# A chunked linear recurrence with an MLP mixer behind it: the recurrence rewritten for quarter tiles of TensorE

## The chip, the cores and the metric

One core of one Trainium2 chip. The time is what the device takes for one execution, in microseconds (us), the lower the better. Engines are named as in the profile: PE is TensorE (PEld its weight load), DVE is VectorE, ACT is ScalarE, POOL is GpSimd, SP is SyncE, which issues most transfers.

## The reference

For each of 4 batches and 8 heads a 40x40 state runs over 768 tokens. The outputs of the heads, side by side, are the input of an MLP mixer.

```python
B, H, S, D = r.shape                      # 4, 8, 768, 40
for t in range(S):
    y[:, :, t] = np.einsum('bhd,bhde->bhe', rt, state)
    Sa = np.einsum('bhde,bhe->bhd', state, at)
    state_decay = state * wt[:, :, None, :] - np.einsum('bhd,bhe->bhde', Sa, bt)
    state = state_decay + np.einsum('bhd,bhe->bhde', vt, kt)

x = y as (B, S, H * D)                    # 320 columns
h = np.maximum(x.transpose(0, 2, 1) @ w_tok1, 0.0) @ w_tok2
u = x + h.transpose(0, 2, 1)
out = u + np.maximum(u @ w_ch1, 0.0) @ w_ch2
```

All inputs and the output are fp32.

## The kernel before

Time is cut into 48 chunks of 64 tokens (g, 12 per batch), heads into four pairs (p). Within a chunk the recurrence is done with matrices. With decays folded into r, a, k and b by cumulated products, the chunk needs the 64x64 lower triangles of A·K and A·B, the inverse T of one plus the second, and from these the outputs and the state that the next chunk starts from. The work is written as generator tasks:

- **t_pre(q)**, once per pair of chunks: cumulated products of w (scans, L443 and L540), multiplied into a (tile AB) and into k and b (tile KBp) by DVE, POOL or ACT (`either`, L370); the correction P of the output; the decay of a whole chunk, PC.
- **t_a(g)**: px (L648) = the products of AB with KBp for two heads at once, a 128x128 matrix whose diagonal 64x64 blocks matter; pa (L614), a transposed by a selection matrix; pk (L270), k and b transposed, evicted into KT and stored to DRAM, from where t_load reads it back as KB. From px come the masked triangle in AT (mask `low`, DVE, L658), and for the inverse the blocks Dg (ACT, L674) and N (L666).
- **t_solve**: inverts the 32x32 diagonal blocks of eight chunks at a time (six sets) on DVE, into TBt and TBn. In the first two sets (`pem=2`) it inverts 16x16 blocks and **merge** (L864, 48 small matmuls a chunk) completes them on PE.
- **t_b(g)**: two products with 32x32 tiles (pe L912, pt L940) complete the 64x64 inverse in TBD, with copies L904 to L906 and L946; ph (L956) multiplies AT by it: HU, evicted by ACT at L961.
- **t_chain(0), t_chain(1)**: the recurrence itself, in two groups of four heads. pq (L1014) goes into a PSUM bank, ACT copies it to G (L1021); four matmuls of HU with G follow, one head after another in one column half (pr, L1027) up to chunk 15, two heads side by side in both halves (pr2, L1033) from chunk 16 on. ACT takes W2s from that (L1070 to L1075), DVE the masked RM (L1043, L1059, L1060, L1065). pS (L1088 and L1089, from chunk 12 on L1097 and L1099 in both halves) gives the new state, DVE multiplies it by PC into the next G (L1107 to L1110), pU (L270) transposes it, ACT copies it to VSs (L1126).
- **t_y**, every second chunk: the outputs of two chunks, L1153 (KB, RM) and L1155 (VSs, RBs), in one PSUM bank yb; DVE multiplies by P (L1185).
- **t_mlp**, once per batch behind its last chunk's output: 1152 records of L1533 and 864 of L1422 in the page are most of it. **t_piece** converts its weights in the first third.

All matmuls of the recurrence are fp32. One fp32 matmul leaves two records in the trace, each with its own weight load. A matmul on fewer rows or columns than 128 uses a tile of the array. What the profile writes as 104\*64 is a matmul with 104 rows, 64 columns.

The order of each engine is static. A planner (class Planner) runs the tasks before the program is built, with a cost for every instruction and a rank (the chunk number less an offset from table K); each engine takes the ready instruction of lowest rank. PSUM banks are rings: three of kind w (evicted by preparation), two of kind c (chain), two of kind m (MLP), one of kind y. On PE the planner inserts filler matmuls (L357, to yb) where too few columns have streamed. All engines thus run a fixed list, and an instruction that waits holds up what is behind it on its engine.

```python
def rank_a(g): ...        # rank of t_a
yield g - K["chain"]      # t_chain, rank of chunk g
yield rank - K["mrg"]     # merge
```

## Time and profile before

| | |
|---|---|
| runs | 937.53, 944.76 and 950.08 us, median 944.76 |
| span of the profiled execution | 933.5 us |
| PE busy | 868.9 us, 93% |
| PEld busy | 807.2 us, 86% |
| DVE busy | 645.8 us, 69% |
| ACT busy | 471.5 us, 51% |
| POOL busy | 256.3 us, 27% |

The time of a run holds some 11 us that lie around the span. Busy time is the union of an engine's instructions; PE's overlap, so their durations do not add up, and what a group costs is read from the start of one group to the start of the next. The granted clock (PEclk) is the share of full speed that PE's clock was allowed.

The program's parts follow each other roughly like this: up to about 100 us the first set is solved; to about 300 us batch 0's recurrence runs beside preparation and weight conversion; then the MLP of one batch runs beside the recurrence of the next; the last product of an output with P starts at 842.8 us, and what follows is the last batch's channel mixing.

### The profile page before, as it was taken

What the parts mean: (1) busy time and instruction counts of PE and PEld (TensorE: products, weight loads), DVE (VectorE), ACT (ScalarE), POOL (GpSimd) and SP (SyncE); (2) the same over time, 40 slices, a digit from 0 to 9 for tenths busy, and PEclk for the clock granted to TensorE, in tenths of its full rate; (3) what the DMA queues carried; (4) which work ended last, traced back from release to release, by engine and by line L of the source; (5) the groups of instructions that cost most, each with busy time, mean ns of one, the idle gap of its engine ahead of it and who ended that gap; (6) DMA issues with size and microseconds to landing.
All of it is one profiled execution on the core that took longest, in us unless ns stands there. A gap on an engine that the chain in (4) does not pass through costs nothing.

```text
span 933.5 us, 28874 instructions
## 1 busy us (share of the span) xinstructions
PE 868.9 (93%) x11662; PEld 807.2 (86%) x11662; DVE 645.8 (69%) x1504; ACT 471.5 (51%) x1501; POOL 256.3 (27%) x335
## 2 busy tenths in 40 slices
PE   4887799998998899999999999999999999998997
PEld 4877697887987888999899888989999999998997
DVE  5789667885888896799836988667975534444443
ACT  2554575655778346546735654554446344433221
POOL 7344533453565312134411121101211111100000
PEclk9788688977999899999859999999999999999999
DMA  5653456547758845454666743644256344335432
GB/s 129 160 163 124 137 166 177 148 120 205 205 178 241 240 128 153 128 131 112 176 179 201 195 138 95 189 106 130 82 172 196 122 117 136 85 101 166 167 99 84
DMA packets 134100, 139.59 MB, mean 150 GB/s; under 512 B 84360, under 2 KB 116872, under 8 KB 130888
## 3 DMA queue, kind: packets, MB, share of 16 engines
q1 hardware_dynamic: 127624, 90.47, 35.3%
q0 software_dynamic: 6336, 47.19, 15.8%
q8 instruction: 95, 1.56, 0.7%
q14 instruction: 45, 0.37, 0.1%
HBM read 111.08 MB, written 26.54 MB: 147 GB/s over the span
## 4 chain that ended last, share of the span: by engine, by line
PE 67%; DMA 11%; DVE 8%; issue 6%; POOL 3%; ACT 3%; SPq 1%; POOLq 0%; DVEq 0%; ACTq 0%
PE m L1422 15%; PE m L1533 13%; DMA w<-in_wT_dram 5%; PE px L648 4%; PE ph L956 4%; PE pq L1014 4%; PE pa L614 4%; PE pq L1033 3%; PE yb L1153 2%; PE yb L1155 2%; PE pt L940 2%; PE pk L270 2%; PE pq L1027 2%; PE pe L912 2%; PE pm L864 2%
## 5 line engine op out<-in xcount | busy, mean ns | idle before, releaser
L1533 PE MATMUL m<-ut,wg_c 128*128 128x256 f32 x1152 | 176.9, 295 | 0.4 <-DVE hd L1545 0.2
L1533 PEld LDWEIGHTS m<-ut,wg_c 128*128 128x128 f32 x1152 | 151.6, 193 | 4.7 <-DVE x L1573 0.4
L1422 PE MATMUL m<-wg_c,hd 128*128 128x320 f32 x864 | 152.3, 317 | 2.7 <-DVE hd L1545 2.3
L1422 PEld LDWEIGHTS m<-wg_c,hd 128*128 128x128 f32 x864 | 128.0, 188 | 6.1 <-DVE hd L1545 3.5
L1543 ACT ACTIVATE hd<-m 128x256 fp32r<-128x256 f32 x144 | 55.3, 384 | 123.8 <-PE m L1533 122.8
L1545 DVE SCALAR_TENSOR_TENSOR hd<-m,hd 128x256 fp32r<-128x256 f32 x144 | 60.6, 421 | 62.1 <-ACT hd L1543 61.8
L906 POOL COPY TBD<-TBt 32x128 f32<-32x128 f32 x86 | 43.9, 510 | 165.7 <-PE ph L956 118.6
L1573 DVE TENSOR_TENSOR x<-m,x 128x320 f32<-128x320 f32 x96 | 46.8, 487 | 53.0 <-PE m L1422 52.5
L370 POOL TENSOR_TENSOR cv_c<-cv_c 128x320 f32<-128x320 f32 (+3 forms) x63 | 61.9, 997 | 69.9 <-ACT cv_c L1257 51.6
L674 ACT ACTIVATE Dg<-px 128x128 f32<-128x128 f32 x144 | 56.1, 390 | 21.0 <-PE px L648 19.2
L1014 PE MATMUL pq<-RBs,VSs 104*104 104x128 f32 x384 | 65.6, 301 | 0.8 <-POOL VSs L1000 0.7
L1043 POOL TENSOR_TENSOR RM<-G,upp 64x128 f32<-64x128 f32 x43 | 22.8, 534 | 143.5 <-ACT G L1021 113.0
L956 PE MATMUL ph<-TBD,AT 128*104 128x128 f32 x384 | 59.2, 299 | 0.9 <-ACT TBD L946 0.6
L648 PE MATMUL px<-KBp,AB 104*128 104x128 f32 x384 | 58.3, 301 | 1.8 <-DVE AT L607 1.6
L1014 PEld LDWEIGHTS pq<-RBs,VSs 104*104 104x104 f32 x384 | 53.6, 188 | 2.5 <-POOL VSs L1000 0.9
L648 PEld LDWEIGHTS px<-KBp,AB 104*128 104x128 f32 x384 | 52.7, 212 | 2.8 <-DVE AT L607 1.8
L1356 POOL DMA_DIRECT2D wg_c<-sG x32 | 18.0, 564 | 131.3 <-PE m L1533 58.4
L956 PEld LDWEIGHTS ph<-TBD,AT 128*104 128x104 f32 x384 | 50.4, 186 | 3.6 <-ACT TBD L946 1.0
L443 DVE TENSOR_TENSOR_SCAN w<-w,D 104x512 f32<-104x512 f32 x24 | 35.1, 1461 | 25.9 <-DMA w<-in_wT_dram 25.9
L614 PE MATMUL pa<-sel,AB 104*128 104x40 f32 x384 | 52.0, 288 | 0.0
L614 PEld LDWEIGHTS pa<-sel,AB 104*128 104x128 f32 x384 | 51.4, 208 | 0.2
L1153 PE MATMUL yb<-KB,RM 128*64 128x40 f32 x768 | 51.3, 235 | 0.0
(179 smaller groups left out, 1980.2 us busy)
## 6 DMA issues: line engine op xcount, KB each, us to landing
wg_c<-sG POOLq DMA_DIRECT2D x16, 1152.0 KB, 6.1
wg_c<-sG POOLq DMA_DIRECT2D x16, 960.0 KB, 5.3
KBp<-in_kbT_dram SPq DMA_DIRECT2D x24, 416.0 KB
wg_t<-sT POOLq DMA_DIRECT2D x8, 1152.0 KB, 6.1
sKB<-KT SPq DMA_DIRECT2D x48, 160.0 KB
KB<-sKB SPq DMA_DIRECT2D x48, 160.0 KB
wr<-in_wT_dram SPq DMA_DIRECT2D x24, 208.0 KB
w<-in_wT_dram SPq DMA_DIRECT2D x24, 208.0 KB
```

The lines of the kernel that those rows point to most:

```text
L370: return [(e, Port(60 + f * n / 0.96 if e == "DVE" else 140 + 2.24 * n), lambda e=e: engines[e].tensor_tensor(out=out_(), in0=a_(), in1=b_ ...
L614: return ("PE", (109, 208, "A"), lambda: nc.tensor.matmul(d["pa"][:, p, :], lhsT=ab[:, p, :], rhs=sel, start=True, stop=True))
L648: nc.tensor.matmul(d["px"][:, p, :], lhsT=ab[:, p, :], rhs=KBp[q][:, p, z, :], start=True, stop=True)
L674: return ("ACT", 190 if sl.start == 0 else 392, lambda: nc.scalar.activation(out=Dg[sl, :, ci * NP:(ci + 1) * NP].rearrange("p s n -> p n s"),
L956: nc.tensor.matmul(d["ph"][0:DP, p, :], lhsT=at[:, p, :], rhs=d["tbd"][:, p, :], start=True, stop=True)
L1014: nc.tensor.matmul(d["pq"][0:DP, 2 * p:2 * p + 2, D:DP], lhsT=vs[:, gi * 2 + p, :], rhs=rb[:, gi * 2 + p, :].rearrange("p (h t) -> p h t", ...
L1153: nc.tensor.matmul(dst, lhsT=rms[g - 1 + z][:, h, :], rhs=o["kb"][:, h, :], start=True, stop=False)
L1422: nc.tensor.matmul(d[key], lhsT=lhs(i, a_), rhs=rhs(i, b_), start=i == 0 and j == 0, stop=i == n - 1 and j == 2)
L1533: nc.tensor.matmul(pt, lhsT=mm_[q][0], rhs=mm_[q][1], start=q == 0, stop=q == len(mm_) - 1)
L1543: nc.scalar.activation(out=hid[key][:, 0], in_=pt, func=AF.Relu)
L1545: now = yield [("DVE", dve(256), lambda: nc.vector.scalar_tensor_tensor(out=hid[key][:, 1], in0=pt, scalar=0.0, in1=hid[key][:, 0].bitcast ...
L1573: now = yield [("DVE", dve(320), lambda: tt(out=x()[:, i], in0=d[("c2", g, i)], in1=x()[:, i], op=ALU.add))]
```

## The change

The recurrence is written in another form, for all eight heads at once. For a chunk with the state S:

- Z = X·V (xv, L991 of the new kernel) + A·S (as_, L1000), both into one bank of kind c, with X the masked triangle. Its negative ZS is evicted by ACT (L1016) or DVE (L1018).
- U = T·Z (L1030) and its transpose (L1033), in two banks of kind c. U goes into the tile W beside V (L1042 on ACT, L1043 on DVE), its transpose to UT (L1106).
- S update (sm, L1057) from KB and W; DVE adds the old state (L1072) and multiplies by PC (L1076; at a batch's first chunk one multiplication, L1070). pu (L1085) transposes the state, evicted into SS (L1092).
- RM (rr, L1122): products of V and U transposed with r, in two banks of kind w, masked by DVE (L1133), two instructions of 128x256 a chunk.
- y (L1168 and L1171) on four column tiles of 32; the first chunk of a batch has no state term.

So pa, ph and HU, pq and G, W2s, RBs, VSs and the matrices idS, low, uppn and PC2 are gone. px (L658) works once per pair of chunks on tiles of 64 rows and 32 columns, eight matmuls per chunk and head pair, into two banks; the mask is applied to the product (XT, L670, one DVE instruction of 128x512). pe and pt run once per pair of chunks, pe (L928) writing its result twice, pt (L943) with a copy by the identity (L946); TBD is evicted in one instruction (L951 or L952) with a masked copy of TBt by POOL or ACT (L909 to L912). Odd heads lie in the other half of the partitions, so the host lays out a, r, v and k, b padded, and a, r and v come in one transfer each. The merge remains for the first set only (pem=1). PSUM banks are allocated once and cleared at the start (L339), and `banks` takes two of a ring at once. Table K of the planner has new numbers throughout. The MLP's code is unchanged.

Matmuls of the recurrence, records halved: px 1536 (192 before), pe 768, pt 768, xv 384, as_ 352, U and its transpose 384 each, sm 352, pu 352, rr 768, y 1472, merge 384 (768 before).

```diff
         def px(z, p):
             def f():
-                nc.tensor.matmul(d["px"][:, p, :], lhsT=ab[:, p, :], rhs=KBp[q][:, p, z, :], start=True, stop=True)
-            return ("PE", (218, 512, "A"), f)
+                ab = AB[q]
+                for i in range(2):
+                    for hf in range(2):
+                        for r in range(2):
+                            rs = rows(r)
+                            rhs = ab[rs, p, z]
...
+                            o0 = i * 64 + hf * 32
+                            nc.tensor.matmul(d["px"][0 if i == r else 1][0][o0:o0 + 32, z, p, :],
+                                             lhsT=KBp[q][rs, p, z, i, hf * 32:hf * 32 + 32], rhs=rhs, start=True, stop=True)
...
+        def pe(n):
             def f():
-                q0, q1 = h * 64, h * 64 + 32
-                nc.tensor.matmul(d["pe"][q0:q0 + L, p, :], lhsT=n21[q1:q1 + L, p, :],
-                                 rhs=TBt[q1:q1 + L, :, ci * NP + p], start=True, stop=True)
+                for dup in range(2):
+                    for b in range(2):
+                        s0, o0 = slice(b * 64, b * 64 + L), b * 64 + (1 - dup) * L
+                        nc.tensor.matmul(d["pe"][o0:o0 + L, n, :], lhsT=o["n21"][s0, n, :], rhs=TBn[s0, n0 + n, :], start=True, stop=True)
...
-    def t_chain(gi):
+    def t_chain():
+        for g in range(NG):
...
+            def xv(p):
+                def f():
+                    for r in range(2):
+                        b = 1 - r
+                        nc.tensor.matmul(d["z"][b * 64:b * 64 + 64, p, :], lhsT=oq["xt"][r * 64:r * 64 + 64, z, p, :],
+                                         rhs=o["w2"][r * 64:r * 64 + 64, 2 * p + r, :], start=p == 0, stop=c == 0 and p == NP - 1,
+                                         skip_group_check=True)
+                return f
+
+            def as_(p):
+                def f():
+                    for r in range(2):
+                        b = 1 - r
+                        nc.tensor.matmul(d["z"][b * 64:b * 64 + 64, p, :], lhsT=AB[q][rows(r), p, z, :],
+                                         rhs=ST[g][rows(r), p, :], start=False, stop=p == NP - 1, skip_group_check=True)
+                return f
...
+            def uu(p):
+                def f():
+                    for r in range(2):
+                        bs = slice((1 - r) * 64, (1 - r) * 64 + 64)
+                        nc.tensor.matmul(u_[bs, p, 0:D], lhsT=oq["tbd"][bs, z, p, :], rhs=d["zs"][bs, p, :], start=True, stop=True)
+                    for r in range(2):
+                        bs = slice((1 - r) * 64, (1 - r) * 64 + 64)
+                        nc.tensor.matmul(t_[rows(r), p, :], lhsT=d["zs"][bs, p, :], rhs=oq["tbd"][bs, z, p, :], start=True, stop=True)
+                return f
...
+            def sm(p):
+                def f():
+                    for r in range(2):
+                        nc.tensor.matmul(d["s"][rows(r), p, :], lhsT=o["kb"][:, 2 * p + r, :], rhs=o["w2"][:, 2 * p + r, :], start=True, stop=True)
+                return f
...
+        def rr(p):
+            def f():
+                for src, hf in (("vt", 0), ("ut", 1)):
+                    for r in range(2):
+                        o0 = 64 * (r ^ hf)
+                        lhs = o["vt"] if hf == 0 else d["ut"]
+                        nc.tensor.matmul(bk[r][0][o0:o0 + 64, p, :], lhsT=lhs[rows(r), p, :],
+                                         rhs=o["rb"][rows(r), p, r * 64:r * 64 + 64], start=True, stop=True)
+            return f
...
+                            if part == 0:
+                                nc.tensor.matmul(dst, lhsT=RMs[gz][:, h, hf * 32:hf * 32 + 32], rhs=o["kb"][:, h, :], start=True, stop=zero)
+                            else:
+                                t1 = r * 64 + hf * 32
+                                nc.tensor.matmul(dst, lhsT=o["rb"][:, p, t1:t1 + 32], rhs=SS[gz][:, p, :], start=False, stop=True)
```

How the new order looks on PE. A piece of the list before, in batch 0's recurrence: the preparation of one chunk (pk, px, pa) and the chain's pq and pr.

```order
L270 MATMUL pk_2853<-ident,KBp_2566 128x104 x4
L648 MATMUL px_2854<-KBp_2566,AB_113 128x128 x4
L614 MATMUL pa_2788<-sel,AB_113 128x40 x4
L1014 MATMUL pq_1_2780<-RBs_131,VSs_137 104x2x64
L1027 MATMUL pq_0_2775<-G_2590,HU_2547 64x104 x4
```

And of the new list, PE through one chunk of the chain; bkc and bkw are banks of the kinds c and w. Ahead of the piece stands rr.

```order
L1122 MATMUL bkw_118<-RB_6963,UT_7291 64x64
L991 MATMUL bkc_122<-W_6841,XT_4211 64x40 x8
L1000 MATMUL bkc_122<-ST_7385,AB_3725 64x40 x8
L1030 MATMUL bkc_121<-ZS_7447,TBD_6778 64x40 x2
L1033 MATMUL bkc_122<-TBD_6778,ZS_7447 40x64 x2
```

The pair of L1030 and L1033 stands there four times, and then:

```order
L1085 MATMUL bkw_120<-sel,ST_7088 40x40 x8
L1085 MATMUL bkw_119<-sel,ST_7385 40x40 x8
L276 MATMUL bkw_118<-ident,KBp_6648 128x104 x4
L1057 MATMUL bkc_121<-W_6841,KB_6981 40x40 x8
L1168 MATMUL yb<-KB_6496,RM_7327 32x40
```

Four 128x128 matmuls became eight small ones each, and the chain's matmuls stand directly behind each other with the evictions of ZS and W between them, which run on other engines.

On DVE, in the same part of the program, before: RM and the state products of the two groups stand between conversions of the MLP's weights (cv_c).

```order
L1065 TENSOR_TENSOR RM_3140<-pq_0_3101,upp 128x256
L1252 TENSOR_SCALAR cv_c_1_1_3137<-cv_c_1_1_3137 128x320
L1065 TENSOR_TENSOR RM_3140<-pq_1_3142,upp 128x256
L370 TENSOR_TENSOR cv_c_1_0_3075<-cv_c_1_0_3075 128x320
L1110 TENSOR_TENSOR G_3146<-pS_0_3186,PC_130 40x4x40
L1110 TENSOR_TENSOR G_3146<-pS_1_3210,PC_130 40x4x40
```

In the new list DVE masks RM from its two banks, with a decay product of KBp between, and makes the state in two steps (L1072, L1076), with conversions between those too.

```order
L1133 TENSOR_TENSOR RM_3718<-bkw_120,upp 128x4x64
L391 TENSOR_TENSOR KBp_3333<-KBp_3333,wr_3304 104x1024
L1133 TENSOR_TENSOR RM_3718<-bkw_118,upp 128x4x64
L1072 TENSOR_TENSOR ST_3748<-bkc_122,ST_3466 104x160
L1265 TENSOR_SCALAR cv_c_1_1_2989<-cv_c_1_1_2989 128x384
L1076 TENSOR_TENSOR ST_3748<-ST_3748,PC 104x160
L391 TENSOR_TENSOR cv_c_1_1_2989<-cv_c_1_1_2989 128x384
L670 TENSOR_TENSOR XT_3839<-bkw_120,upp 128x512
```

The state now passes DVE twice and may stand behind a conversion in between.

## Rows read from the trace of the kernel before

**Rows 1.** The page, part 1: busy time, share of the span, instructions.
```profile
PE 868.9 (93%) x11662; PEld 807.2 (86%) x11662; DVE 645.8 (69%) x1504; ACT 471.5 (51%) x1501; POOL 256.3 (27%) x335
```

**Rows 2.** Two stretches: length, busy PE, PEld, DVE, ACT, POOL; clock, DMA share, GB/s.
```profile
0.00:300.00 300.00, 259.50 (x4369) 237.09 (x4369) 229.07 (x489) 176.56 (x532) 140.87 (x152) 0.86 0.59 164
300.00:842.00 542.00, 527.39 (x6668) 489.34 (x6669) 379.49 (x929) 273.54 (x907) 110.65 (x175) 0.96 0.50 145
```

**Rows 3.** The second stretch: busy PE and PEld of L648, then of L1033 alone.
```profile
300.00:842.00 542.00, 25.63 (x176) 23.33 (x176) 0.96 0.50 145
...
300.00:842.00 542.00, 32.41 (x512) 24.70 (x512) 0.96 0.50 145
```

**Rows 4.** Short stretches, columns as in rows 2: the clock stands third from the end.
```profile
98.00:99.20 1.20, 1.14 (x65) 1.07 (x66) 1.20 (x5) 0.69 (x2) 0.00 (x0) 0.50 0.61 178
178.00:184.50 6.50, 6.50 (x115) 5.95 (x113) 5.76 (x10) 5.47 (x18) 0.00 (x0) 1.00 0.82 228
186.00:200.00 14.00, 11.26 (x298) 10.38 (x297) 12.33 (x22) 6.44 (x19) 6.66 (x8) 0.63 0.37 104
406.00:411.00 5.00, 5.00 (x133) 4.63 (x132) 4.61 (x13) 1.76 (x7) 2.33 (x1) 1.00 0.01 4
420.00:422.00 2.00, 2.00 (x37) 1.65 (x36) 1.77 (x6) 1.41 (x6) 0.00 (x0) 1.00 0.81 170
```

**Rows 5.** PE's timeline near 180 us: start, duration, line, tile and records.
```profile
179.34 1.16 PE L648 MATMUL px<-KBp,AB 104*128 104x128 f32 x8
180.33 0.98 PE L614 MATMUL pa<-sel,AB 104*128 104x40 f32 x8
181.14 1.10 PE L1014 MATMUL pq<-RBs,VSs 104*104 104x128 f32 x8
182.17 0.62 PE L912 MATMUL pe<-TBt,N 32*32 32x32 f32 x16
182.73 0.93 PE L1027 MATMUL pq<-G,HU 104*64 104x104 f32 x8
183.58 0.22 PE L864 MATMUL pm<-TBt,N 32*32 32x32 f32 x1
...
183.97 0.23 PE L864 MATMUL pm<-TBt,N 32*32 32x32 f32 x1
```

**Rows 6.** PE's timeline near 408 us.
```profile
406.30 0.64 PE L940 MATMUL pt<-ET,TBn 32*32 32x32 f32 x16
406.88 0.28 PE L1097 MATMUL pS<-W2s,KB 128*40 128x40 f32 x4
...
407.52 0.29 PE L1153 MATMUL yb<-KB,RM 128*64 128x40 f32 x4
...
409.49 0.60 PE L270 MATMUL pU<-sel,G 40*40 40x40 f32 x8
410.01 1.12 PE L956 MATMUL ph<-TBD,AT 128*104 128x128 f32 x8
410.89 1.20 PE L1533 MATMUL m<-ut,wg_c 128*128 128x256 f32 x8
```

**Rows 7.** PE's timeline near 420 us.
```profile
420.25 0.93 PE L1033 MATMUL pq<-G,HU 104*64 104x104 f32 x16
421.11 0.62 PE L912 MATMUL pe<-TBt,N 32*32 32x32 f32 x16
```

**Rows 8.** PE's timeline near 98 us.
```profile
98.06 0.68 PE L864 MATMUL pm<-ET,TBn 32*32 32x32 f32 x32 [1.42 <-DVE ET L871]
98.54 0.64 PE L864 MATMUL pm<-TBn,ET 32*32 32x32 f32 x32
99.11 1.14 PE L357 MATMUL yb<-ident 128*128 128x192 bf16 x6
```

**Rows 9.** DVE by line and shape: count, busy us, mean ns, idle time before.
```profile
L658 DVE TENSOR_TENSOR AT<-px,low 128x256 f32<-128x256 f32 x48 | 19.9, 417 | 9.1 <-ACT Dg L674 4.5 <-PE pU L270 2.2 <-ACT noff L666 1.7
L1110 DVE TENSOR_TENSOR G<-pS,PC 40x160 f32<-40x160 f32 x22 | 7.0, 327 | 6.0 <-PE pS L1089 5.6
```

## Prediction before the run

> **What bounds the kernel now.** I read the page's busy shares first. TensorE is busy 93% of the span, VectorE 69%, ScalarE 51%, GpSimd 27% [rows 1]. A share of 93% can still hide stretches with other limits, so the second view is a table of two, cut where the work changes: up to 300 us the recurrence of batch 0 runs beside preparation and weight conversion, up to 842 us recurrence and MLP share the engines; behind that only the MLP of batch 3 is left, 92 us in which nothing of the change runs. From 300 to 842 us TensorE is busy 527 of 542 us at a mean granted clock of 0.96 [rows 2]: there a microsecond of TensorE is a microsecond of the span. Before, it is busy 259.5 of 300 us and VectorE 229, so there VectorE is close behind.
>
> The third view says which chunks fall where: of the px matmuls 176 of 384 records lie behind 300 us, so 22 chunks of 48 are prepared there; of the chain's pair form (L1033) all 512 records, which with one chunk still in the form of L1027 makes 33 chunks of recurrence [rows 3].
>
> A fp32 matmul leaves two records. TensorE's records overlap, so a group's price is read from its start to the start of the next group, in stretches at full clock [rows 4].
>
> **What is removed.** From such starts [rows 5]: px 0.99 us a chunk, pa 0.81, pq 1.03, pe 0.56, and one group of four heads in one column half (L1027) 0.85. From a later stretch [rows 6]: pt 0.58, pS 0.64, y 1.97 for two chunks, 0.98 for one, pU 0.52, ph 0.88. Eight records of L1027 take 0.85, the sixteen of L1033, in both column halves, 0.86 [rows 7]: two tiles beside each other double the rate, and a round, in which each tile does one matmul, takes 0.107. Together that is 7.85 us a chunk in the pair form; pk and ptr stay.
>
> **What is added.** Two bounds price it. The first is the round: 0.107 for L1033, 0.12 for y (weights 64 wide, sixteen rounds in 1.97), 0.08 for pS (weights 40 wide, eight rounds in 0.64). The second is how fast the engine starts matmuls at all. The fastest group of the trace is pm, on four tiles of 32 rows: 32 records, so sixteen matmuls, from 98.06 to 98.54, 30 ns each, at a granted clock of 0.50 [rows 4, 8]; at clock 1.00 28 records lie between 183.58 and 183.97, 28 ns for a matmul [rows 4, 5]. The clock makes no difference to it, so I read it as a limit of starting, and take the larger bound for each group:
> - Z: xv four rounds on two tiles, 0.115 each, 0.46; as_ the same on 44 of 48 chunks, 0.42.
> - U and its transpose (L1030 and L1033 of the new kernel): sixteen matmuls, four rounds of four quarter tiles, 0.48, and by starts the same. rr likewise, 0.48.
> - sm and pu: weights 40 wide, four rounds of 0.08 on 44 of 48, 0.28 each.
> - pe and pt: sixteen matmuls a chunk each, 30 ns, 0.48 each.
> - px: 32 matmuls a chunk on eight tiles; four rounds would be 0.48, by starts 0.96.
> - y: 31 matmuls a chunk on four column tiles; by rounds of 0.08 0.62, by starts 0.92.
>
> For px and y no row shows so many tiles; I take the starts, because pm is the nearest row, and keep the rounds for the range. Changing the tile form: the second pm group takes 0.57 up to what follows it where the first took 0.48 [rows 8], so 0.1 a change. The old prices hold theirs already; the new groups change form about eight times a chunk (px, pe and pt come once in two), 0.8, or nothing if a change is free. New groups 5.24 + 0.8 = 6.04, against 7.85.
>
> **Do quarter tiles run beside each other?** That carries the sum, and only part of it has a row. Column halves do [rows 7]. Of row tiles, pe uses two and takes 0.56 for eight matmuls, 70 ns each [rows 5]; pm uses four, all writing one PSUM bank, and takes 30 [rows 8]. Twice the tiles, 2.3 times the rate: they work at once, in one bank. [...] What no row shows is two row tiles that share columns, as px, uu and rr have them (the kernel gives those different banks).
>
> **The other engines.** VectorE loses for a chunk, in the form of the first 16 chunks, the mask of AT (417 ns), two RM products of the same 128x256 (417 each) and two G products (327 each) [rows 9]: 1.9 us. It gains half of a 128x512 XT product (0.42 by the same row), two RM products of 128x256 (0.83) and two passes over ST of 160 elements (0.65): 1.9 us again, so it keeps its 229 us in the first 300. ScalarE loses G, HU, four VSs copies and narrow copies of pe and pt and gains ZS, W, UT and SS: fewer instructions on an engine that is busy 274 of 542 us. It binds nothing. GpSimd loses the TBD copies and SyncE two transfers a chunk.
>
> **The sum, by stretch.**
> - Up to 300 us: TensorE would save px and pa of 26 chunks (0.84 each, 22), the rest of 16 (1.77 each, 28, and 14 more because L1027 runs two groups of 0.85 there), eight merges of 48 matmuls (12), less 16 x 0.8 for changes: 63, at the clock of 0.86 [rows 2] 73 us, down to 227. VectorE's 229 us come first: busy 90% of the time (it is 12.3 of 14 us where it is densest [rows 4]) they make 250. **Minus 50**; nothing, if its order stays as loose as now; at most 73.
> - 300 to 842 us: px and pa 22 x 0.84 = 18; pq, L1033, pS, pU, ph, pe, pt and y are 6.05, their successors 4.28, 33 x 1.77 = 58; changes 33 x 0.8 = 26. Net 50, at clock 0.96 **minus 52**.
> - New waits: Z goes through an eviction, U through another, ST through two VectorE instructions before the next Z. With 1.6 us of matmuls and five instructions of about a third of a microsecond that is some 3.3 us of chain a chunk, where the stretch has 15. MLP matmuls fill the gaps; I take a quarter of a microsecond a chunk uncovered, 33 x 0.25 = **plus 8**. Without that cover it is the third rival.
> - Behind the last y: nothing.
>
> 933.5 - 50 - 52 + 8 = 839.5 us of span. Around the span lie 944.8 - 933.5 = 11.3 us (the median of the runs against the profiled execution): **851 us**.
>
> **Rivals.**
> 1. *Quarter tiles that share columns take turns.* uu and rr grow by 0.96 a chunk (px is at the bound of starts anyway): 32 us at clock 0.96, plus 33, 884. No row excludes it.
> 2. *All row tiles take turns*, and the change does not do what it says: xv, as_, uu, pu and rr double, 2.12 a chunk. From 300 us on 33 x 2.12 = 70 stand against 50, 21 us more than now by the clock; the first stretch still saves 63 - 34, 34 us. 933.5 + 21 - 34 + 8 + 11 = 940, no change. [...]
> 3. *The chain binds.* Seven steps a chunk, on three engines that work in a planned order. If each chunk needs 16.9 us where my sum has 498 / 33 = 15.1: plus 60, 911. For it: VectorE is 70% busy, so an eviction can stand behind long instructions. Against: the chain of before has as many steps, and TensorE hardly waits for it.
> 4. *Slower: the granted clock falls*, from 300 us on. Between 186 and 200 us it is 0.63 while TensorE is busy 11.3 of 14 us, with short tiled matmuls [rows 4]; the new kernel has many more of those and fewer that fill the array. The 498 us of that stretch are 478 at full clock; at 0.70 they take 683, 1036 in all. Below a mean of 0.78 the kernel is slower by over 2%. Against: much of that stretch is the MLP's full tiles, untouched, and it ran at 0.96.
>
> **Chances.** Side by side as worked out 0.62, with a range of its own from 785 (px and y by rounds, 21 less; changes free, 27 less; the rest from the first stretch) to 895 (half or none of the first stretch's 50, longer waits). Rival 1 0.08, rival 2 0.06, rival 3 0.12, rival 4 0.12. Two per cent is about what a measurement of this kernel can tell from no change; the marks are 926 and 964. Faster 0.62 + 0.08 + 0.12 = 0.82; within, rival 2, 0.06; slower, rival 4, 0.12. From 785 to 925 lie all but rivals 2 and 4.
>
> **What the changed profile would show.** At clock 1.00 the sum wants xv's eight matmuls within 0.5 us, uu's and rr's sixteen within 0.5 each, px's 64 of a pair within 2, y's of a pair within 1.9. If uu takes 0.9 and xv 0.46 it is rival 1; if xv takes 0.9, rival 2; px in 1.0 a pair, and the limit of starts is wrong in the kernel's favour. The chain is covered if TensorE stays over 93% busy from 300 us to the last y; below 88%, with ZS, W or ST as releasers, it is rival 3. A granted clock under 0.9 there points to rival 4. The first stretch is right if the preparation of chunk 26 ends near 250 us with VectorE about 90% busy up to it. Behind the last y there should be 92 us again; anything else is an error for which I have no term.

## The result, and the profile after

The new kernel takes 884.55 us, median of four runs (881.29 to 892.76); the kernel before took 942.91 in the runs beside it. Ratio 0.939, with an interval from 0.932 to 0.946: faster, by 58 us where 94 were forecast, inside the range of 785 to 925. The profiled execution spans 879.4 us, where my sum had 839.5. So the direction held, and 40 us of the expected gain are missing. The rest of this document is about where they went. One figure ahead of the prediction is wrong: a run is not 11 us longer than its span but about 2 (881.29 against 879.4 here, and much the same in every run that has both on record). The rest of the 11.3 us that the forecast put around the span is the distance between the profiled execution of the kernel before and the median of its runs.

First the page's busy line [rows 1], and part 2's row of the granted clock, of before and of after (40 slices, tenths):

```profile
PE 766.4 (87%) x18765; PEld 684.7 (78%) x18765; DVE 568.3 (65%) x1308; ACT 281.7 (32%) x824; POOL 174.3 (20%) x183
```
```profile
PEclk9788688977999899999859999999999999999999
```
```profile
PEclk9675555656678999899559999789999999999999
```

TensorE has 61% more records and is busy 103 us less. Its idle time has risen: 933.5 - 868.9 = 65 us before, 879.4 - 766.4 = 113 after. That is the first sign: the work went, and about half of what went came back as waiting. The clock row shows a second: from the fourth slice to the thirteenth, some 65 to 285 us, it stands mostly at 0.5 to 0.6 where it stood at 0.7 to 0.9.

Next the stretches, cut at the same two points of the work in both kernels: batch 0's last output (L1185 before, at 275.9; L1195 after, at 243.2), and the last output of all (842.8 and 786.7). Columns as in rows 2; before:

```profile
0.00:276.00 276.00, 236.83 (x4010) 216.63 (x4011) 208.69 (x441) 157.34 (x473) 129.43 (x140) 0.85 0.57 161
276.00:843.00 567.00, 551.06 (x7052) 510.75 (x7051) 400.29 (x978) 292.75 (x965) 122.09 (x186) 0.96 0.51 148
```

And after:

```profile
0.00:243.00 243.00, 186.59 (x5896) 160.12 (x5896) 171.80 (x382) 84.49 (x236) 89.97 (x83) 0.62 0.60 177
243.00:787.00 544.00, 495.39 (x12251) 441.84 (x12243) 358.62 (x837) 175.06 (x523) 79.08 (x90) 0.92 0.55 170
787.00:879.00 92.00, 84.47 (x629) 82.76 (x627) 37.88 (x90) 22.14 (x65) 5.30 (x10) 0.98 0.41 133
```

Batch 0 is done 33 us earlier (my sum had 50 for about that stretch), the next stretch is 23 shorter (I had 44 net), the tail is 92 as forecast. In both stretches TensorE is idle more than before: 23% against 14%, and 9% against 3%. VectorE, which was to bound the first one at 90%, is busy 71%.

Most prices came out. TensorE's timeline of the new kernel at full clock (start, duration, line, tile and records; start to next start is the price):

```profile
404.64 0.23 PE L1122 MATMUL bkw<-RB,UT 40*64 40x64 f32 x2
404.70 0.61 PE L991 MATMUL bkc<-W,XT 64*64 64x40 f32 x16
405.14 0.64 PE L1000 MATMUL bkc<-ST,AB 40*64 40x40 f32 x16
406.19 0.25 PE L1030 MATMUL bkc<-ZS,TBD 64*64 64x40 f32 x2 [0.40 <-ACT ZS L1016]
...
406.67 0.79 PE L1085 MATMUL bkw<-sel,ST 40*40 40x40 f32 x32
...
407.96 0.51 PE L1057 MATMUL bkc<-W,KB 128*40 128x40 f32 x16
408.40 0.28 PE L1168 MATMUL yb<-KB,RM 128*32 128x40 f32 x8
...
459.63 0.86 PE L658 MATMUL bkw<-AB,KBp 40*32 40x64 f32 x64
460.42 0.38 PE L1543 MATMUL bkm<-ut,wg_c 128*128 128x256 f32 x1
...
690.26 0.27 PE L1122 MATMUL bkw<-RB,VT 40*64 40x64 f32 x2
...
690.77 0.47 PE L1085 MATMUL bkw<-sel,ST 40*40 40x40 f32 x16
```

xv takes 0.44 us (0.46 in my sum, before the 0.1 for a change of form), uu 0.48 from 406.19 to 406.67 (0.48), rr 0.51 (0.48), sm 0.44 (0.32 and a change), px 0.79 for a chunk (0.96). The rows of xv, uu and rr are among the shortest of their kind, with no change of form behind them. Most full-clock groups of xv and uu take 0.59 and of rr 0.62, which is my price with the 0.1 of a change. At the lower clock it is 0.95 to 1.02 for most of xv, 1.02 for most of uu and 0.92 to 1.06 for most of rr.

The groups that I priced by the limit of starting came out otherwise. First a pair's y, a pair's pe and a typical xv at clock 1.00, each with what follows it, then pe at clock 0.50:

```profile
280.46 0.28 PE L1168 MATMUL yb<-KB,RM 128*32 128x40 f32 x8
...
281.79 0.31 PE L991 MATMUL bkc<-W,XT 64*64 64x40 f32 x4
...
330.20 0.75 PE L928 MATMUL bkw<-TBn,N 32*32 32x32 f32 x64
330.89 0.50 PE L1543 MATMUL bkm<-ut,wg_c 128*128 128x256 f32 x2
...
353.65 0.66 PE L991 MATMUL bkc<-W,XT 64*64 64x40 f32 x16
354.24 1.22 PE L1543 MATMUL bkm<-ut,wg_c 128*128 128x256 f32 x8
```
```profile
179.50 1.07 PE L928 MATMUL bkw<-TBn,N 32*32 32x32 f32 x64
180.50 0.33 PE L1030 MATMUL bkc<-ZS,TBD 64*64 64x40 f32 x2
```

The 64 matmuls of y take 1.33 us, 21 ns each, and pe's 32 take 0.69, 22 ns each, where I had 28 to 30. At the lower clock pe takes 1.00, 31 ns each.

### The profile page after: what moved, and what is told of

Same layout as the page of the kernel before. It is cut to its first block, busy times and chain, and to the rows that moved or that the text cites. A ratio compares the mean times of both kernels' runs of the same rounds, so it can differ in the third digit from the quotient of the medians.

```text
span 879.4 us, 41673 instructions
## 1 busy us (share of the span) xinstructions
PE 766.4 (87%) x18765; PEld 684.7 (78%) x18765; DVE 568.3 (65%) x1308; ACT 281.7 (32%) x824; POOL 174.3 (20%) x183
## 4 chain that ended last, share of the span: by engine, by line
PE 61%; issue 15%; DMA 11%; DVE 9%; ACT 2%; SPq 1%; POOL 1%; ACTq 0%; POOLq 0%; DVEq 0%
PE bkm L1432 11%; PE bkm L1543 10%; PE bkc L1432 4%; PE bkw L1543 4%; PE bkw L1122 3%; PE bkw L658 3%; PE bkw L276 3%; PE bkc L1030 3%; DMA sX<-P 3%; PE bkc L991 3%; PE bkc L1000 2%; PE yb L1168 2%; PE bkc L1057 2%; DMA w<-in_wT_dram 2%; PE yb L378 2%
## 5 line engine op out<-in xcount | busy, mean ns | idle before, releaser
L1543 PE MATMUL bkm<-ut,wg_c 128*128 128x256 f32 x760 | 122.8, 303 | 2.2 <-issue 1.6
L1543 PEld LDWEIGHTS bkm<-ut,wg_c 128*128 128x128 f32 x760 | 103.2, 199 | 7.2 <-issue 2.0
L1432 PE MATMUL bkm<-wg_c,hd 128*128 128x320 f32 x558 | 101.1, 324 | 7.2 <-issue 4.7
L1432 PEld LDWEIGHTS bkm<-wg_c,hd 128*128 128x128 f32 x558 | 83.8, 191 | 11.2 <-issue 5.2
L1133 DVE TENSOR_TENSOR RM<-bkw,upp 128x256 f32<-128x256 f32 x96 | 38.9, 417 | 25.2 <-PE bkw L1122 24.6
L1543 PE MATMUL bkw<-ut,wg_c 128*128 128x256 f32 x392 | 54.7, 286 | 0.4 <-DVE hd L1555 0.4
L1543 PEld LDWEIGHTS bkw<-ut,wg_c 128*128 128x128 f32 x392 | 50.3, 189 | 1.0 <-DVE hd L1555 0.5
L378 PE MATMUL yb<-ident 128*128 128x192 bf16 x291 | 48.0, 330 | 3.0 <-POOL ident masks.py:199 2.7
L912 POOL TENSOR_SCALAR TBD<-TBt,blk 128x256 f32<-128x256 f32 x17 | 20.0, 1176 | 150.1 <-PE bkw L1085 48.6
L1122 PE MATMUL bkw<-RB,VT 40*64 40x64 f32 x768 | 43.2, 258 | 6.7 <-DMA KB<-sKB 3.2
L1168 PE MATMUL yb<-KB,RM 128*32 128x40 f32 x1536 | 42.0, 222 | 7.7 <-issue 6.4
L1168 PEld LDWEIGHTS yb<-KB,RM 128*32 128x32 f32 x1536 | 36.2, 125 | 13.7 <-issue 10.2
L658 PE MATMUL bkw<-AB,KBp 40*32 40x64 f32 x2560 | 38.5, 258 | 9.1 <-issue 6.2
L1122 PEld LDWEIGHTS bkw<-RB,VT 40*64 40x64 f32 x768 | 34.6, 162 | 14.2 <-issue 5.3
L1030 PE MATMUL bkc<-ZS,TBD 64*64 64x40 f32 x768 | 40.1, 254 | 6.0 <-ACT ZS L1016 3.7
L1030 PEld LDWEIGHTS bkc<-ZS,TBD 64*64 64x64 f32 x768 | 33.3, 161 | 15.4 <-issue 7.6
```

Of the source, the lines that this page charges most:

```text
L378: nc.tensor.matmul(yb[:, 320:512], lhsT=zf[:, 0:128], rhs=zf[:, 0:192], start=True, stop=True)
L658: nc.tensor.matmul(d["px"][0 if i == r else 1][0][o0:o0 + 32, z, p, :], lhsT=KBp[q][rs, p, z, i, hf * 32:hf * 32 + 32], rhs=rhs, start=Tru ...
L1030: nc.tensor.matmul(u_[bs, p, 0:D], lhsT=oq["tbd"][bs, z, p, :], rhs=d["zs"][bs, p, :], start=True, stop=True)
L1122: nc.tensor.matmul(bk[r][0][o0:o0 + 64, p, :], lhsT=lhs[rows(r), p, :], rhs=o["rb"][rows(r), p, r * 64:r * 64 + 64], start=True, stop=True)
L1133: tt(out=RMs[g].rearrange("p (n h) t -> p n h t", h=2)[:, :, r, :], in0=bk[r][0], in1=upp.unsqueeze(1).to_broadcast([128, NP, C]), op=ALU. ...
L1168: nc.tensor.matmul(dst, lhsT=RMs[gz][:, h, hf * 32:hf * 32 + 32], rhs=o["kb"][:, h, :], start=True, stop=zero)
```

## Where TensorE waits now

TensorE's own waits in the new kernel, costliest first (line, what it waited for, us in total, times, longest):

```profile
PE bkc L1057 <- issue: 6.4, 3, 3.1
PE yb L1168 <- issue: 6.4, 6, 1.9
PE bkw L658 <- issue: 6.2, 5, 2.9
PE bkw L928 <- issue: 5.3, 2, 3.2
PE bkw L868 <- DVE TBn L812: 4.9, 1, 4.9
PE bkm L1432 <- issue: 4.7, 1, 4.7
```

"Issue" is time in which the engine waited for nothing that the profile shows. Over all lines it comes to 59.9 us in 44 places; before it was 3.6 in 2. The lines have nothing in common, and the pauses fall into the middle of groups, as here, inside one chunk's px:

```profile
453.45 1.15 PE L658 MATMUL bkw<-AB,KBp 40*32 40x64 f32 x61
455.29 0.42 PE L658 MATMUL bkw<-AB,KBp 40*32 40x64 f32 x3 [0.69 <-issue]
```

I therefore numbered TensorE's instructions in the order in which they start (weight loads, matmuls and its sequencer's own) and looked where pauses of more than a quarter microsecond begin. In the new kernel 42 of 84 begin at a number of the form 256 n + 192, give or take one, and these make 61.1 us; in the kernel before it is 2 of 40, 4.0 us. Part 3 of the page has a queue that fits; before, then after (packets, MB, share):

```profile
q8 instruction: 95, 1.56, 0.7%
```
```profile
q8 instruction: 149, 2.44, 1.2%
```

Each packet has 16,384 bytes, and TensorE has 23,324 and 37,530 weight loads and matmuls: one packet for about 250 of them, some 64 bytes each. The times of these packets fit too: each of the 42 pauses ends 1.2 to 1.7 us after one of them has landed. So the theory to test is: **TensorE's instructions come in blocks of 256 by DMA, and a stretch of small matmuls uses a block up before the next has arrived** (theory F in what follows). Rival S: the only limit is the 28 ns a fp32 matmul (four instructions, 7 ns each) that the prediction took from pm, and the missing time is elsewhere. Rival C: the granted clock, 0.62 in the first stretch where it was 0.85, costs the missing time.

## Experiments

**1. Instruction supply by itself.** A kernel with nothing but matmuls of two sizes, with and without transfers beside them (A is a constant tile, ws the tiles that the transfers fill).

```python
def small(n, t, bank):
    for i in range(n):
        for q in range(4):
            sl = slice(q * 32, q * 32 + 32)
            c0 = (i % 8) * 32
            nc.tensor.matmul(pa[bank][sl, c0:c0 + 32], lhsT=t[sl, 0:32], rhs=t[sl, 32:64], start=True, stop=True)
...                                        # large: one matmul of 128x128 by 256 each
for i, t in enumerate(ws):                 # 28 transfers of 104 x 1024
    nc.sync.dma_start(out=t[0:104], in_=kbT[i % 24])
large(24, A, 0); small(192, ws[0], 1); large(160, A, 0); small(192, A, 2); large(24, A, 0)
...                                        # 24 stores of the output
```

> A stand-alone stream on TensorE; it computes nothing of the reference (the output is zeros). 24 large fp32 matmuls (128x128 by 256), then 768 small ones (32x32 by 32 on four diagonal tiles) while SyncE's transfers of 28 x 416 KB run, then 160 large ones, then 768 small ones without transfers, then 24 large ones. Theory F (instruction supply): TensorE's instructions come in blocks of 256 (64 fp32 matmuls are 256 instructions: two weight loads and two matmuls each) and small matmuls use a block up faster than the next arrives. Then the small stretches show pauses of 0.5 to 3 us at every 64th matmul, so a block takes 3.5 to 5 us instead of 1.8, the 768 take 42 to 60 us, longer beside the transfers than without, and the large stretches show none. Rival S (only the 7 ns from start to start): no pauses, 768 matmuls in about 22 us in both stretches.

TensorE's timeline of it:

```profile
14.25 1.67 PE L269 MATMUL p<-w 32*32 32x32 f32 x175
18.59 1.27 PE L269 MATMUL p<-w 32*32 32x32 f32 x128 [2.67 <-issue]
26.70 1.93 PE L269 MATMUL p<-w 32*32 32x32 f32 x128 [6.84 <-issue]
35.09 1.93 PE L269 MATMUL p<-w 32*32 32x32 f32 x128 [6.46 <-issue]
43.21 1.93 PE L269 MATMUL p<-w 32*32 32x32 f32 x128 [6.19 <-issue]
...
82.35 70.53 PE L273 MATMUL p<-A 128*128 128x256 f32 x320
152.81 2.20 PE L269 MATMUL p<-A 32*32 32x32 f32 x239
157.64 1.27 PE L269 MATMUL p<-A 32*32 32x32 f32 x128 [2.63 <-issue]
161.09 1.93 PE L269 MATMUL p<-A 32*32 32x32 f32 x128 [2.18 <-issue]
164.55 1.93 PE L269 MATMUL p<-A 32*32 32x32 f32 x128 [1.52 <-issue]
168.00 1.93 PE L269 MATMUL p<-A 32*32 32x32 f32 x128 [1.52 <-issue]
```

And its stretches (busy PE, PEld, DVE, POOL; clock, DMA share, GB/s):

```profile
15.00:65.00 50.00, 11.83 (x879) 10.94 (x865) 0.00 (x0) 0.00 (x0) 0.55 0.85 221
153.00:195.00 42.00, 21.26 (x1537) 19.76 (x1526) 0.00 (x0) 0.00 (x0) 0.58 0.02 4
```

Behind the first of each stretch, every pause comes after exactly 128 records, which with their weight loads are 256 instructions. Without transfers a block takes 3.5 us (161.09, 164.55, 168.00) to 4.0; beside the loads of ws, at a DMA share of 0.85, it takes 8.1 to 8.4 (26.70, 35.09, 43.21). The engine itself needs 1.3 us for it at full clock (157.64) and 1.9 at the lower one, to which the granted clock fell behind the first pauses (1.00 at 157 us, 0.50 at 161). The large matmuls, where a block lasts 28 us, show no pause. S is wrong here: a small matmul costs not 28 ns but 54 on the average (3.45 us for 64), and 127 beside the loads (8.1 for 64). Where I had the 768 matmuls at 42 to 60 us, they took 68 with transfers (14.25 to 82.35) and 42 without (152.81 to 194.78).

The amount of traffic alone does not decide it. From 65.6 to 73.6 us the output's stores run at 220 to 250 GB/s, as much as the loads, with a DMA share of 0.65 to 0.73, and there a block takes 3.7 and 4.3 us (from 65.6 to 69.4 and 73.6). The packets of q8 tell where the time goes. Beside the loads a packet takes 1.2 to 1.3 us, without transfers mostly 0.9 to 1.1. But without transfers it starts up to 0.9 us before the engine stops, and beside the loads 3.4 to 4.1 us after (the engine stops at 19.86, the packet runs from 23.92 to 25.20, the engine goes on at 26.70). Loads come mostly in packets of 4,096 bytes, stores in packets of 1,280; whether this, the direction or the share makes the difference, no run shows.

**2 to 4. Fewer instructions for the same product.** Three edits of the new kernel that leave every order as it is.

```diff
# y in two column tiles of 64 (e2, e4)
-                                nc.tensor.matmul(dst, lhsT=RMs[gz][:, h, hf * 32:hf * 32 + 32], rhs=o["kb"][:, h, :], start=True, stop=zero)
+                            nc.tensor.matmul(dst, lhsT=RMs[gz][:, h, :], rhs=o["kb"][:, h, :], start=True, stop=zero)
...
# px in four tiles of 64x64 (e3, e4); Dg and noff are then evicted in three pieces
-                    for hf in range(2):
-                        for r in range(2):
...
+                    for r in range(2):
+                        nc.tensor.matmul(d["px"][0 if i == r else 1][0][i * 64:i * 64 + 64, z, p, :],
+                                         lhsT=KBp[q][rs, p, z, i, :], rhs=ab[rs, p, z], start=True, stop=True)
...
# pe without the second copy (e4)
-                for dup in range(2):
+                for dup in range(1):
```

> The new kernel with its output matmuls on two column tiles of 64 instead of four of 32: 736 matmuls instead of 1472, 2944 TensorE instructions fewer of 37530, everything else and every order the same. In the two traces y takes 52 us of TensorE's time before (64 wide) and 43 in the new kernel (32 wide). Theory F: the 9 us more of matmul time are given back by 11 or 12 blocks of instructions fewer at 0.4 to 0.9 us of pause each; 876 to 886, and TensorE's idle time for issue falls by about 5 us from 60. Rival S: nothing is given back; 890 to 895, idle time for issue unchanged. Rival C (the lower granted clock is what holds the new kernel back): no change of idle time, clock as before, 884 to 892.

> The new kernel with px on four tiles of 64x64 instead of eight of 64x32: 768 matmuls instead of 1536, 3072 instructions fewer; ScalarE gets two more evictions of 64 partitions' worth per pair of chunks for the diagonal blocks (about 0.8 us a pair). Theory F: matmul time of px from 44 to about 23 us, and 12 blocks fewer at 0.4 to 0.9 us: 850 to 865. Rival S: px's own 21 us less where TensorE is the bound (two thirds of it): 868 to 874, idle time for issue unchanged. Rival C: as S or less.

> Both edits together, and pe no longer writes the second copy of its result, which nothing reads: 7552 instructions fewer of 37530, 20%. Theory F: px -21, pe -10, y +9 of matmul time and 29 blocks fewer at 0.4 to 0.9 us; 840 to 860, idle time for issue from 60 to under 48. Rival S: 862 to 872 with the idle time for issue at 60. Rival C: the same as S, and if the lower TensorE use costs more clock, 875 to 890 with a mean clock under 0.82.

Times and sums worked out of the traces. "Matmul time" is the sum over TensorE's records of the time from a start to the next start, less the idle time between; "block ends" are the pauses at 256 n + 192. Both belong to the profiled execution. Ratios are against runs of the kernel before on the same chip; the median of the kernel before lay between 937.6 and 954.4 us beside these runs, on several chips, so compare the ratios rather than the times.

| kernel | blocks (q8) | matmul time | all idle | of it block ends | time | ratio and interval |
|---|---|---|---|---|---|---|
| before | 95 | 868.6 | 57 | 4 | 942.91 | 1 |
| after | 149 | 766.1 | 104 | 61 | 884.55 | 0.939 (0.932 to 0.946) |
| e2, y 64 wide | 138 | 789.2 | 81 | 37 | 879.36 | 0.937 (0.930 to 0.944) |
| e3, px 64x64 | 137 | 766.9 | 106 | 35 | 881.85 | 0.933 (0.923 to 0.942) |
| e4, both and pe | 120 | 775.8 | 78 | 12 | 868.27 | 0.926 (0.919 to 0.933) |
| e9, e4 with y 32 wide | 131 | 770.3 | 92 | 24 | 861.96 | 0.914 (0.908 to 0.921) |
| e10, e4 without late fillers | 119 | 765.7 | 82 | 9 | 860.02 | 0.913 (0.906 to 0.921) |
| e11, e9 without late fillers | 130 | 755.5 | 102 | 23 | 868.29 | 0.922 (0.914 to 0.930) |
| e12, e9 without fillers | 129 | 731.2 | 117 | 27 | 865.15 | 0.921 (0.913 to 0.929) |

The pauses at block ends follow the number of instructions: 61 us, then 37 and 35 with some 3,000 instructions fewer, 12 with 7,500 fewer. That is F; S and C have no reason for it. TensorE's waits for issue, all lines together, fall likewise from 59.9 to 37.0, 33.9 and 16.0. What became of the time was another matter. In e2 y takes 60.9 us of matmul time against 43.0 (I had 52), since a pair that takes 2.00 us at clock 1.00 takes 3.57 at 0.50, and this eats most of the 24 us of pauses; the time lies in F's range, and so does after's. In e3 px takes 37.7 against 44.1 (I had 23), and while 26 us of pauses at block ends are gone, other idle time grew by 28: TensorE's wait for ZS, for one, from 3.7 to 10.1 us, probably since ScalarE now evicts Dg in three pieces. My 850 to 865 for e3 was a miss. e4 lost 49 us of pauses and gained 16 in time (12 by the ratios), 868 where I gave F 840 to 860: its matmul time is 10 us above that of after, because of y (pe saved 2 where I had 10), and its other idle time is higher by 23. So the supply of instructions is shown as the cause of the pauses. That taking the pauses away gives their whole length back is not shown: in e4 other waits came up in their place.

TensorE's two largest waits in e4 are named instructions again:

```profile
PE bkc L1028 <- ACT ZS L1014: 7.7, 10, 2.1
PE bkw L866 <- DVE TBn L810: 7.0, 1, 7.0
```

**5 and 6. More fillers.** `fill_cols` 4800 instead of 3550 in e4 (e5); 6000 in the first 250 us of the plan (e6).

> The lean kernel (e4) with filler matmuls up to 4800 columns instead of 3550 in the planner's count: 552 fillers instead of 291, so 522 TensorE instructions more (two blocks). Theory C (in 100 to 250 us it is the granted clock, 0.52 in e4, that keeps batch 0's recurrence slow): the clock of that stretch rises to 0.7 or more, batch 0's last output comes 8 us or more earlier, 850 to 860. Theory F (instruction supply alone): clock may rise, but blocks come no faster; 866 to 872, output times unchanged.

> The lean kernel with fillers up to 6000 columns in the first 250 us of the plan and as before behind it: 864 fillers instead of 291, 1146 instructions more (4 to 5 blocks), some 48 us of TensorE time in planned gaps at full clock. Theory C: clock of 100 to 250 us 0.8 or more, batch 0's last output 10 to 25 us earlier, 840 to 855. Theory F: the added instructions cost 4 blocks of 4 to 8 us in a stretch that waits for blocks anyway: 870 to 885 whatever the clock. If VectorE were what bounds that stretch, as my prediction had it, neither: 864 to 872 and VectorE busy the same share.

888.91 (0.938, 0.929 to 0.946) and 897.07 (0.945, 0.935 to 0.955), both outside every range. e6 is slower than e4; e5's interval overlaps with e4's. The clock from 100 to 240 us rose from 0.52 to 0.58 and 0.70. But the two edits also moved other work: the planner counts fillers as time and orders the rest anew, and between the fourth and fifth output of e5 there are 51 us where e4 has 23. They do not tell C from F.

**7 and 8. The same, with the order kept.** Fillers are put ahead of every second change of tile form between 95 and 245 us of the plan, without the planner counting them.

```diff
+                if ns[2] != self.form and self.filler is not None and 95e3 < t0 < 245e3 and t0 > self.hold + 1500.0:
+                    self.extra += 1
+                    for _ in range(3 * (self.extra % 2 == 0)):      # 6 in e8
+                        self.filler[3]()
```

> The lean kernel (e4) with its order on every engine kept, and three filler matmuls put ahead of every second change of tile form on TensorE between 95 and 245 us of the plan: 126 fillers more, 252 instructions, about 10 us of TensorE at full clock and 42 changes of form at 0.1 us. In e4 the small groups of that stretch take twice the time that they take at full clock (rr 1.06 us, xv 1.01). Theory C: the granted clock of 100 to 240 us goes from 0.52 to 0.7 or more, groups take half, batch 0's last output at 215 to 228 us instead of 235, 848 to 862 in all. Theory F: groups take half but the blocks of instructions don't come faster, the idle time for issue in that stretch grows by what the groups lose: last output 233 to 245 us, 866 to 880.

> As e7 with six fillers at each place: 252 more, 504 instructions (two blocks), 21 us of TensorE at full clock. Theory C: clock of 100 to 240 us 0.85 or more, batch 0's last output at 210 to 225 us, 845 to 860. Theory F: as e7 or later by two blocks of 4 to 8 us: 245 us, 872 to 885.

878.38 (0.934, 0.926 to 0.942) and 870.92 (0.926, 0.917 to 0.935). The clock of 100 to 235 us went from 0.53 to 0.56 and 0.63 only, so neither theory got the condition that it was to be judged by. e7's time lies in F's range, e8's one us below it. Batch 0's last output came at 242.5 and 241.5 instead of 235.3, as F had it, but with block ends at 7 and 11 us in all, where F wanted them to grow: TensorE waits less and works longer, filler time 64 and 77 us instead of 43. So far no more than: fillers at this price buy nothing.

**9. y back on four tiles.** e4 without the edit on y.

> The lean kernel (e4) with y back on four column tiles of 32, as in the new kernel: 2944 TensorE instructions more than e4. By the traces y takes 43 us of TensorE's time that way and 61 in e4. Theory F: the 18 us of matmul time are taken back by 11 to 12 blocks of instructions, idle time at block ends 30 to 40 us where e4 has 17; 862 to 874, no gain over e4's 868. Rival S: 848 to 856.

861.96, ratio 0.914 where e4 has 0.926, with intervals that touch. Block ends 24 us against 12, other idle time about the same, matmul time of y 42.6 against 61.3. F expected the two to cancel, S a gain of 12 to 20 us; the median is at F's lower end, a gain of a per cent. (The profiled execution has a span of 871.8 us, so its sums in the table are those of a longer one than the median.)

**10 to 12. Fewer fillers.** A filler of the plan is left out, its place in the plan kept, so the order of everything else stays: behind 95 us in e4 (e10) and in e9 (e11), all of them in e9 (e12).

```diff
-        self.issue(fn, (0, 0, 0, "PE", 0, fn, (self.run_(),), None), now, ns)
+        if now < 95e3:
+            self.issue(fn, (0, 0, 0, "PE", 0, fn, (self.run_(),), None), now, ns)
```

> The lean kernel without the 102 fillers behind the first 95 us of the plan, everything else in the same order: 204 instructions and some 18 us of TensorE time less. Theory C (the clock is worth its price): the granted clock from 240 to 780 us falls from 0.92 under 0.88, in 100 to 240 us it stays near 0.5; 872 to 890. Theory F (a matmul that isn't issued is time won, the clock matters little): clock down by 0.02 or less, 852 to 866.

> e9's form (px on 64x64 tiles, no second copy of pe, y on four column tiles) without the fillers behind 95 us of the plan, as in e10. If the two savings add up, as theory F has it (fillers cost TensorE time and blocks, clock unchanged): 850 to 860, ratio to before about 0.905. If the fillers do hold the clock where matmuls are small (theory C): clock 0.48 to 0.50 in 100 to 240 us and under 0.90 behind it, 862 to 875.

> e11 without any filler at all: 189 more removed, all in the first 95 us, 28 us of TensorE time in a stretch in which VectorE is busy 80% and TensorE waits for it. Theory C: the clock of 0 to 100 us falls from 0.7 to 0.5 and batch 0's outputs come 5 to 15 us later; 858 to 872. If VectorE sets that stretch, as my prediction had it for all of the first 300 us: clock falls and the outputs stay where they are, 850 to 860 as e11.

e10: 860.02, 0.913, inside F's 852 to 866; the clock from 240 to 760 us is 0.92 with the late fillers and 0.92 without. They bought nothing. e11 does not add the two savings up: 868.29 lies in the range that I gave to C, but the clock, 0.51 from 100 to 240 us and 0.91 behind, did not fall as C's condition wanted. Its interval overlaps with those of e9 and e10; at this size the runs no longer tell versions apart. e12, without a single filler, is as fast as e11. Its first stretch needs care in reading. Page part 2 gives it a full clock there:

```profile
PEclk9999999656557999897579899989999999999999
```

but its groups contradict that row. Here px (64 records) and pk (4) of e12, and then the same px of e11 in a stretch at full clock:

```profile
39.65 1.99 PE L652 MATMUL bkm<-AB,KBp 40*64 40x64 f32 x64
41.56 0.95 PE L275 MATMUL bkw<-ident,KBp 104*128 104x104 f32 x4
```
```profile
41.10 1.16 PE L654 MATMUL bkm<-AB,KBp 40*64 40x64 f32 x64
42.19 0.57 PE L277 MATMUL bkw<-ident,KBp 104*128 104x104 f32 x4
```

1.91 us against 1.09: at 40 us e12 runs at the lower clock (at 28.57 us, at a granted clock of 0.50, e11's px takes 1.92 too). Its trace has no record of the clock before 145 us, and the row shows full clock for want of one. So it is in the new kernel's trace, whose first record of the clock begins at 18.7 us: the row shows full clock ahead of it, though L276 takes 0.95 us there (at 9.31), as at 29.16 at a clock of 0.50, and 0.58 at 40.62 at a clock of 1.00. So without fillers batch 0 began at half clock, and still its first two outputs came at 121.4 and 144.7 us, where e11 with 189 fillers has 124.1 and 145.2. Up to 100 us the two are alike for VectorE, the busiest engine there (busy PE, PEld, DVE, ACT, POOL; the clock of the second row is the one that is not to be trusted):

```profile
0.00:100.00 100.00, 68.20 (x1410) 58.54 (x1410) 78.47 (x170) 45.54 (x111) 40.34 (x37) 0.72 0.58 166
```
```profile
0.00:100.00 100.00, 49.47 (x1266) 41.72 (x1268) 80.39 (x174) 46.27 (x115) 40.38 (x38) 1.00 0.61 171
```

VectorE is busy 78 and 80 us in both; TensorE's 19 us less became idle time. So up to 145 us the lower clock and the missing fillers together cost nothing that these runs can measure. Behind it e12 draws ahead (last output of batch 0 at 229.5 us against 236.2), but from 160 to 240 us its clock is the higher one, 0.59 against 0.50, so there C is not excluded. As to the ranges, 865.15 lies in the one that I gave C, though the outputs came earlier and not later; the other range was written around an e11 of 850 to 860.

## Why the prediction was right, and where its sum was not

*TensorE as the bound.* Right for the recurrence behind batch 0: from 300 us to the last output TensorE is busy 449 of 487 us, 92%, between my marks of 93 and 88. Of the 37 us in which it waited, 25 were waits for issue; ZS and W, which rival 3 would have named, made 2.5. For each kernel of the table matmul time and idle time add up to the span less the 8 to 16 us ahead of TensorE's first matmul and behind its last, and the gain from before to after is 868.6 - 766.1 = 102 us of matmul time less 104 - 57 = 47 us of added idling.

*Quarter tiles run beside each other.* Right, also for tiles that share columns, for which no row stood: rr, whose row tiles share columns, does sixteen matmuls in 0.51 us, and uu in 0.48. Rival 1 would have shown 0.9 for both, rival 2 0.9 for xv. Two row tiles that write one bank do not take turns either: xv has two such tiles, and its eight matmuls take 0.44 us, 55 ns each, where turns at 0.115 would make 0.92.

*The prices.* Right within a tenth for xv, uu and rr at full clock. One reading behind them was wrong without harm: the eight matmuls of L1033, on two tiles in 0.86 us, are four rounds of 0.215 and not eight of 0.107. For xv I took 0.115, near y's 0.12, which is a round read rightly. The 28 to 30 ns that I took for px, y, pe and pt, as a limit on which the clock has no effect, is none: at full clock px, y and pe take 21 to 25 ns a matmul, at the lower clock px and pe 31 and y about 40. In sum TensorE's matmul time fell by 102 us where my two stretches had 73 and 52 at their clocks; 12 of the difference are fillers and MLP matmuls, which took 6 us more each (39.4 to 44.9, 343.2 to 349.4).

*The step that failed* is that limit of starting: "The second is how fast the engine starts matmuls at all". I took it from a group of 32 records, 64 instructions, a quarter of a block, and let it stand for runs of many blocks; the change has 7,904 matmuls. Over a whole block the rate is another: in experiment 1 256 instructions in 3.5 us at best, 54 ns a fp32 matmul, and less than half of that rate beside loads. The new kernel needs 149 blocks instead of 95 and waits 61 us at their ends where the kernel before waited 4. Of the 61, 29 fall before 240 us and 32 behind. Two readings agree on the block's size: q8's packets of 16,384 bytes, one for about 250 instructions, and the pauses after 128 records, which with their weight loads are 256. Its time is from experiment 1. What was missing from the prediction was the count: 14,000 instructions more on TensorE, 56 blocks.

Behind batch 0 this is what my sum missed. There matmul time fell by 56 us (551.1 to 495.0; I had 52), but idle time rose by 33 (15.9 to 48.6; I had 8), 32 of them at block ends, and I was 21 us short. In the first stretch the account is another. Idle time rose by 17 us (39.2 to 56.4), less than the 23 that my own sum implied up to its cut at 300 us (73 us of TensorE's time saved, 50 of the span), although 29 us of pauses are in it. What is missing there is matmul time: 50 us saved (236.8 to 186.8) of 73, at a granted clock of 0.62 where my sum kept 0.86. So there the failed term is that clock, and whether the 17 us came from it stays open.

*VectorE bounds the first stretch at 250 us.* Wrong in its reason, though batch 0 ends near there (243). VectorE is busy 71% up to 243 us, not 90, because its work fell too: 172 us up to batch 0's last output where the kernel before has 209, and not the same as I had claimed from five instructions a chunk. The preparation of chunk 26, whose end I wanted near 250 us, ends at 295.8 (286.1 before): the new order does it later, so that sign failed too. At most up to 100 us does VectorE set the pace (about 80% busy, and without fillers, in e12, the first outputs came no later).

*The granted clock.* Rival 4 looked for it from 300 us on, where it fell little (0.92). It fell in the first stretch, to 0.62. After the experiments its price stays open: no edit raised it by much without changing something else, and where fillers were taken away nothing was lost. That groups take 1.4 to 1.9 times as long at half clock is plain (px of e12 and e11 1.91 against 1.09, pe 1.00 against 0.69, y of a pair some 2.5 against 1.33); whether full clock would have shortened that stretch is not, since the blocks of instructions would then have been used up sooner and VectorE is busy 71% there.

*The chain.* Not the bound: TensorE's waits for ZS come to 4.2 us in the new kernel, those for W, ST, SS and RM to 4.1. The term of 8 us for new waits was about right.

*The tail.* 92 us, as said.

## What to carry to other kernels

Count instructions, not only columns and rounds: a fp32 matmul is four of them on TensorE (two records, each with its weight load), and a dense run of small matmuls was supplied here at one block of 256 in 3.5 to 8.4 us, whatever the array could do, so split into smaller tiles only where that saves array time, and keep large matmuls between the small ones for the blocks to arrive behind: in e1 a block of large ones lasted 28 us, and TensorE did not pause in them. Where a profile names "issue" as what a busy engine waited for, see whether the pauses come at equal numbers of instructions. Try a kernel without its fillers: here they took 45 us of TensorE time, and the kernel without them (e12, 0.921, against e9, 0.914, and e11, 0.922) lost nothing that could be told from noise.

## What the runs showed of the hardware

- Blocks of 256 TensorE instructions arrive every 3.5 to 4.0 us with the transfer engines idle, and every 8.1 to 8.4 beside loads at a DMA share of 0.85 (221 GB/s), but every 3.7 to 4.3 beside stores at 0.65 to 0.73 (220 to 250 GB/s); small fp32 matmuls on four tiles use a block up in 1.3 at full clock and 1.9 at half (e1). In the new kernel 42 pauses of TensorE end 1.2 to 1.7 us after such a block has landed.
- Row tiles that share columns, writing different banks, work at once: at full clock 16 matmuls on tiles of up to 64x64 in 0.48 (uu) to 0.51 us (rr), where turns would have made 0.9. Two row tiles that write one bank do too: eight matmuls in 0.44 us (xv), where turns at 0.115 would have made 0.92.
- Eight tiles of 64x32 start a fp32 matmul every 25 ns at full clock, the change of form included (px); four column tiles of 32 start one every 21 ns at clock 1.00 (y).
- The row of the granted clock can show full clock where the trace has no record yet: in e12 up to 145 us, with px at 1.91 us, 1.75 times the 1.09 that it takes at full clock in e11, and in the new kernel up to 18.7 us, with L276 at 0.95 us against 0.58 at a clock of 1.00.
